# A recurrence feeding a GELU MLP: half of the inverse decay powers as ScalarE products, the decays' transfer issued by ScalarE, and one bonus half moved to VectorE

## The chip, the cores and the metric

The kernel runs on one core of a Trainium2 chip. The time is device time in microseconds (us) from the first to the last instruction of one launch; the median of several launches is compared. All work is in float32; a float32r product is split into a high and a low part, so that three matmuls stand for one.

## The reference

A linear recurrence over 768 positions for 4 batches and 8 heads of 48 channels, and then an MLP of 384 to 2048 to 384 with GELU on the 3072 tokens that come out:

```python
for t in range(S):
    kt, vt, rt = (k[:, :, t], v[:, :, t], r[:, :, t])
    cur = np.einsum('bhd,bhe->bhde', u[None] * kt, vt)
    y[:, :, t] = np.einsum('bhd,bhde->bhe', rt, state + cur)
    state = w[None, :, :, None] * state + np.einsum('bhd,bhe->bhde', kt, vt)
...
h = x @ w_in
g = 0.5 * h * (1.0 + erf(h * inv_sqrt2))
return (g @ w_out).astype(np.float32)
```

## The kernel before

**Tiling.** The 768 positions are cut into 6 chunks of 128. In each chunk the 8 heads go as 4 pairs (in the order 3, 0, 1, 2), so there are 24 groups of one pair and one chunk. Inside a group the recurrence is matrix work: r and k are scaled by positive and negative powers of the decay w (tile Ts for the first four groups, Tb scaled by E for the later ones), their products give scores (bank A or Y in PSUM), the entries of the past are copied by a mask into Am (L489, L670), the diagonal is the bonus u·k·r (RK, cs, then "bonus": L415 on ScalarE, four activations for a half, or L420 on VectorE, one product for a half), and Am times v gives y. Between chunks a state (Sa, Sb) is carried.

**Prologue.** wu_sb holds the decays w and the bonus u. `powers` (L321 to L327, VectorE) makes w^1 to w^64 of all four pairs in W by doubling. `inverse` (L333, VectorE) makes w^-64 to w^-1 of one pair as one reciprocal of 112x64. `state_powers` (L346, L344, ScalarE) makes the powers up to w^128, which are flipped by TensorE into WN (L354, L357). RK is r times k (L465), Ts is T times the powers of W (L459), raw holds the MLP's packed weights, and E (four transfers, L366) is read back out of W.

**MLP.** The 96 steps (6 chunks of 16 blocks of 128 hidden units) each take 9 matmuls of 128x512 into bank Hp (L696; step 1 uses bank O2), two GELU evaluations on ScalarE (gh L728, gf L729), a subtraction on VectorE (gl = gf - gh, L730), and 9 matmuls into the three banks O (L740). "Hp wh" and "Hp wl" are the products with the high and the low part of the weights, three matmuls each. In the first chunk the weights are unpacked beside it, for each step j: wa (L395) and wb (L398) on ScalarE from raw, their sum wb (L400) on VectorE, wh (L404) on ScalarE, wl (L407) on VectorE. "products" of a group (L606 old states, L614 scores A<-Tb, L623 gains A<-Nb, L634 new) is one block on TensorE; the states (L663) on VectorE need its gains, and the next group's block needs those states.

**What sets the order.** Every operation is handed to a class `Plan` with a modelled length, a due time and what it reads and writes. `run` plays a list schedule on these models, engine by engine, the earliest due operation that is ready first, and emits the instructions in that order; the engines then run their own streams in order and wait on semaphores. So any modelled cost, and any operation moved from one engine to another, can move others. All loads go through the queue of SyncE (SP), in the order of the plan; a load waits there for the landing of the load eight before it. `warm_up` puts HEATS matmuls of zeros on TensorE at the start, and the plan puts further such matmuls into modelled gaps until MLP step 0.

Of the kernel before, what the change touches and what calls it, by code (L numbers as in the profile page):

```python
# [9 lines left out]
F32 = mybir.dt.float32  # L10
# [6 lines left out]
AF = mybir.ActivationFunctionType  # L17
# [6 lines left out]
C = 128  # L24
NCH = S // C
PAIRS = (3, 0, 1, 2)
NP = H // 2
NB = B
TOK = NB * C
NJ = DF // 128  # L30
HALF = 64
# [7 lines left out]
LATER = 10 ** 7  # L39
FIRST, STEP, STEP_LAST = 27000, 8400, 3900  # L40
WEIGHT_AHEAD, GROUP_AHEAD, GROUP_DUE = 26000, 28000, 18000
LEFT = 6
HEATS, HEAT_NS, HEAT_ROOM, MM = 10, 300, 100, 233
WIDE = 96
POOL_DUE, POOL_CLASH = 8000, 550
LATER_BONUS = "d"
# [4 lines left out]

SCALE = ("dd", "d", "d", "d")
PRODUCT = ("d", "d", "d", "d")
BONUS = ("aa", "aa", "aa", "ad")


class Plan:
# [6 lines left out]
    LAG = {"pe": 220, "act": 140, "dve": 115, "pool": 90, "sp": 0, "do": 0}  # L64
    DMA_GAP, DMA_LEAD, DMA_FIXED, DMA_LANES = 480, 1050, 950, 8
    DMA_EARLY, DMA_RATES = 5000, (400.0, 345.0)
    DMA_QUEUED, DMA_SPREAD = 1200, 1050

    def __init__(self, after):
        self.after = after  # L70
# [3 lines left out]
    def add(self, eng, ns, at, fn, r=(), w=(), port=False):  # L74
        n = len(self.ops)
        deps = set()
        for x in r:
            deps.add(self.writer.get(x))
            self.readers.setdefault(x, []).append(n)
        for x in w:  # L80
            deps.add(self.writer.get(x))
            deps.update(self.readers.pop(x, ()))
            self.writer[x] = n
        deps -= {None, n}
        self.ops.append((eng, ns, at, fn, deps, port or eng == "pool"))
        self.reads.append(set(r))
        self.writes.append(set(w))
        return n

    def dma(self, nbytes, at, fn, r=(), w=()):  # L90
        self.add("sp", nbytes, at, fn, r, w)
# [18 lines left out]
    def play(self, due):  # L110
# [6 lines left out]
        bus, locked, lanes = 0.0, {"dve": 0.0, "pool": 0.0}, [0.0] * self.DMA_LANES  # L117
# [4 lines left out]
        for _ in ops:  # L122
            best, clash = None, float("inf")
            for e in self.LAG:
# [4 lines left out]
                while wait and wait[0][0] <= start:  # L129
                    n = heapq.heappop(wait)[1]  # L130
                    heapq.heappush(can, (due[n], n))
                if can:
                    n = can[0][1]
                else:
                    start = wait[0][0]
                    n = min((due[n], n) for at, n in wait if at == start)[1]
# [8 lines left out]
            start, e, n = best  # L145
# [14 lines left out]
            if e == "sp":  # L160
                free[e] = start + self.DMA_GAP
                queued = bus - start - self.DMA_LEAD
                bus = max(bus, start + self.DMA_LEAD) + ns / self.DMA_RATES[start >= self.DMA_EARLY]
                end = bus + self.DMA_FIXED + self.DMA_SPREAD * (queued > self.DMA_QUEUED)
                lanes = lanes[1:] + [end]
            else:
                free[e] = end = start + ns
# [23 lines left out]
def rwkv_gelu_mlp(tc, rkT, rkv, wuT, uN, wmlp, r, k, vT, w, u, out):  # L191
    nc = tc.nc
    with ExitStack() as ctx:
# [73 lines left out]
            else:  # L267
                dma(C * 4608, at + 1, lambda: nc.sync.dma_start(N[s], rkv[gi]), r=r, w=[f"Nr{s}", f"Nk{s}", f"Nv{s}"])

        dma(5000, -10 ** 6, lambda: nc.sync.dma_start(wu_sb, wuT), w=["w_sb"])  # L270
        load_group(0, LATER)


# [55 lines left out]
                n *= 2  # L329
            return last  # L330

        def inverse(p0, p1):
            return nc.vector.reciprocal(out=W[:, p0:p1, 0:HALF], in_=W[:, p0:p1, C:HALF:-1])  # L333

        add("dve", 1500, 5, powers, r=["w_sb"], w=["P"], port=True)
        first = PAIRS[0]
        add("dve", 480, 6, lambda: inverse(first, first + 1), r=["P"], w=[f"W{first}"])
        for p in PAIRS[1:]:
            add("dve", 480, LATER, lambda p=p: inverse(p, p + 1), r=["P"], w=[f"W{p}"])


        def state_powers():
# [13 lines left out]
        def flipped(dst):  # L356
            return lambda: nc.scalar.copy(out=dst, in_=O[0].rearrange("s (p j x) -> s p j x", p=NP, x=64)[:, :, :, :D])  # L357

        add("act", 1700, LATER, state_powers, r=["P"], w=["WKs"])
        add("pe", 560, LATER, lambda: flip(lambda p: WKs[:, p, :]), r=["WKs", "ident"], w=["O0"])  # L360
        add("act", 400, LATER, flipped(WN), r=["O0"], w=["WN"])

# [380 lines left out]
        def moe2(m, at, dest):  # L743
# [27 lines left out]
            for i, (d, bank, a, b) in enumerate(parts):  # L771
# [8 lines left out]
                        out=o, in_=bank[:, a:b], mul=256.0), r=[banks[i]], w=[f"{R}{'' if last else i}"])  # L780
                if last:
                    dma(512 * (b - a), at + 2000, lambda d=d, a=a, b=b, o=o: nc.sync.dma_start(dest[d][:, a:b], o), r=[R])
            if not last:
                dma(128 * 6144, at + 20000, lambda: nc.sync.dma_start(
                    dest.rearrange("d p n -> p d n"), flat2(raw[0]).bitcast(F32).rearrange("p (d n) -> p d n", d=3)),
                    w=[f"raw0{i}" for i in range(3)])
# [221 lines left out]
```

## Time and profile before

| what | value |
|---|---|
| median of 3 launches | 478.93 us (478.65 to 478.95) |
| the profiled launch | 478.3 us, of which the profile's span is 476.6 us |
| TensorE busy | 469.2 us, 98% of the span |
| VectorE, ScalarE, GpSimd busy | 230.7, 181.8, 67.6 us |
| granted clock of TensorE | 1.00 |

The profile is of one launch; 1.7 us of it lie outside the span. Rows below name an engine (PE is TensorE's matmuls and PEld its weight loads, DVE VectorE, ACT ScalarE, POOL GpSimd, SPq the queue of SyncE), a line of the kernel, the operation, and the tile written and read. "x4" after a row is a run of four such instructions with no wait between, and the bracket behind a row is the time that the engine stood idle before it and what ended that.

### The profile page before, as it was taken

The page shows a single profiled execution, that of the slowest core. Times are in us where ns is not written, and L with a number is a line of the kernel's source. Part 1 is how long each engine was busy: PE and PEld are TensorE (multiplying, and loading weights), DVE is VectorE, ACT ScalarE, POOL GpSimd, SP SyncE. Part 2 cuts the span into 40 slices and gives each one's busy share as a digit, 9 for nine tenths or more (in the row PEclk, how much of TensorE's full clock was granted, in tenths as well). Part 3 has the DMA queues.
Part 4 walks back from the last instruction along what each step waited for, and adds up shares of the span by engine and source line. Part 5 has one row for each costly group of instructions (what it writes and reads, how often), then busy time and mean ns, then how long its engine had stood idle before and what let it go on. Part 6 is the DMA issues. An engine that isn't in the chain of part 4 may idle for free.

```text
span 476.6 us, 10284 instructions
## 1 busy us (share of the span) xinstructions
PE 469.2 (98%) x4525; PEld 378.3 (79%) x4525; DVE 230.7 (48%) x345; ACT 181.8 (38%) x333; POOL 67.6 (14%) x91
## 2 busy tenths in 40 slices
PE   8999999999999999999999999999999999999996
PEld 6767788888888787888888888888888887888875
DVE  7989989754354266153543543544435311211111
ACT  9998897233222223222223222223322222322221
POOL 1331021221020222010202202202112000000000
PEclk9999999999999999999999999999999999999999
DMA  8978682414023034031231330321402000100002
GB/s 306 362 296 312 231 265 91 122 48 155 25 83 106 2 114 153 1 106 39 69 106 67 96 99 9 106 54 52 162 15 91 14 0 12 66 1 1 1 0 72
DMA packets 15426, 46.60 MB, mean 98 GB/s; under 512 B 3664, under 2 KB 4048, under 8 KB 15376
## 3 DMA queue, kind: packets, MB, share of 16 engines
q1 hardware_dynamic: 15376, 45.88, 28.8%
q8 instruction: 37, 0.61, 0.5%
q14 instruction: 13, 0.11, 0.1%
HBM read 38.73 MB, written 4.72 MB: 91 GB/s over the span
## 4 chain that ended last, share of the span: by engine, by line
PE 92%; DMA 4%; ACT 3%; issue 0%; DVE 0%; ACTq 0%
PE Hp L696 42%; PE O L740 41%; PE Y L606 2%; DMA E<-W 2%; PE A L614 2%; PE Y L634 2%; PE A L623 1%; DMA raw<-in_wmlp_dram 1%; PE Y L740 1%; ACT W L344 0%; ACT Sa L530 0%; ACT wa L312 0%; ACT L291 0%; ACT wa L395 0%; ACT gh L728 0%; ACT gf L729 0%
## 5 line engine op out<-in xcount | busy, mean ns | idle before, releaser
L696 PE MATMUL Hp<-xx,wh 128*128 128x512 f32 x570 | 167.2, 401 | 0.0
L730 DVE TENSOR_TENSOR gl<-gf,gh 128x512 fp32r<-128x512 f32 x92 | 66.9, 727 | 166.4 <-ACT gf L729 166.1
L728 ACT ACTIVATE gh<-Hp 128x512 fp32r<-128x512 f32 x91 | 54.4, 598 | 213.9 <-PE Hp L696 213.8
L696 PEld LDWEIGHTS Hp<-xx,wh 128*128 128x128 f32 x570 | 104.4, 188 | 25.8 <-ACT gf L729 1.5
L696 PE MATMUL Hp<-xx,wl 128*128 128x512 f32 x285 | 82.1, 395 | 0.0
L740 PE MATMUL O<-gh,wh 128*128 128x512 f32 (+1 forms) x276 | 78.6, 391 | 0.5 <-ACT gf L729 0.5
L740 PE MATMUL O<-gh,wl 128*128 128x512 f32 (+1 forms) x276 | 78.6, 391 | 0.0
L740 PE MATMUL O<-gl,wh 128*128 128x512 f32 (+1 forms) x276 | 78.3, 390 | 0.0
L696 PEld LDWEIGHTS Hp<-xx,wl 128*128 128x128 f32 x285 | 53.6, 188 | 12.7
L740 PEld LDWEIGHTS O<-gh,wh 128*128 128x128 f32 x276 | 51.7, 188 | 13.5 <-ACT gf L729 0.9
L740 PEld LDWEIGHTS O<-gh,wl 128*128 128x128 f32 x276 | 51.2, 188 | 11.6
L740 PEld LDWEIGHTS O<-gl,wh 128*128 128x128 f32 x276 | 51.0, 188 | 11.4 <-issue 0.2
L729 ACT ACTIVATE gf<-Hp 128x512 f32<-128x512 f32 x95 | 56.3, 593 | 0.0
L561 POOL TENSOR_TENSOR Nb<-Nb 128x384 f32<-128x384 f32 x20 | 20.4, 1018 | 124.7 <-DMA Nb<-in_rkv_dram 75.4
L558 DVE TENSOR_TENSOR Tb<-Tb,E 112x1024 f32<-112x1024 f32 x20 | 25.4, 1268 | 2.3 <-DMA Tb<-in_rkT_dram 2.3
L663 DVE SCALAR_TENSOR_TENSOR Sb<-Sa,E,A 48x192 f32<-48x192 f32 x40 | 16.5, 413 | 18.1 <-PE A L623 17.5
L433 ACT CAST xx<-Y 112x512 fp32r<-112x512 f32 x15 | 8.8, 587 | 38.8 <-PE Y L634 38.7
L564 POOL TENSOR_TENSOR Nb<-Nb,WN 128x384 f32<-128x384 f32 x20 | 20.3, 1016 | 21.2 <-DVE wl L407 7.8
L567 POOL TENSOR_TENSOR Nb<-Nb,u_sb 128x384 f32<-128x384 f32 x20 | 20.3, 1013 | 17.8 <-DVE gl L730 12.5
L570 DVE TENSOR_REDUCE cs<-Nb 128x8 f32<-128x384 f32 x20 | 11.1, 553 | 18.1 <-POOL Nb L567 15.8
L644 POOL MEMSET done<- 1x1 f32 x19 | 1.7, 89 | 124.6 <-PE Y L606 124.6
L670 DVE COPY_PREDICATED Am<-past,A 128x512 f32<-128x512 uint32 x20 | 14.9, 747 | 7.0 <-PE A L623 6.8
(124 smaller groups left out, 388.9 us busy)
## 6 DMA issues: line engine op xcount, KB each, us to landing
raw<-in_wmlp_dram SPq DMA_DIRECT2D x16, 767.8 KB, 6.6
Nb<-in_rkv_dram SPq DMA_DIRECT2D x20, 576.0 KB, 5.6
Tb<-in_rkT_dram SPq DMA_DIRECT2D x20, 512.0 KB, 4.1
out_dram<-raw SPq DMA_DIRECT2D x5, 768.0 KB, 3.6
T<-in_rkT_dram SPq DMA_DIRECT2D x4, 512.0 KB, 5.0
xx<-x SPq DMA_DIRECT2D x30, 64.0 KB, 4.2
N<-in_rkv_dram SPq DMA_DIRECT2D x4, 384.0 KB, 7.0
out_dram<-raw SPq DMA_DIRECT2D x2, 256.0 KB, 2.1
```

Of the source, the lines that this page charges most:

```text
L558: add("dve", 1140, LATER, lambda: nc.vector.tensor_tensor(out=flat, in0=flat, in1=E[:, p, 0].rearrange("l h i -> l (h i)").unsqueeze(1).to ...
L561: add("pool", pool(DM), LATER, lambda: nc.gpsimd.tensor_tensor(out=n[:, 0], in0=n[:, 0], in1=n[:, 1], op=ALU.mult), r=[NK], w=[NR])
L564: add("pool", pool(DM), LATER, lambda: nc.gpsimd.tensor_tensor(out=kn, in0=kn, in1=WN2[:, p].rearrange("s j d -> s (j d)").unsqueeze(1).to ...
L567: add("pool", pool(DM), LATER, lambda: nc.gpsimd.tensor_tensor(out=n[:, 0], in0=n[:, 0], in1=u_sb[:, p, :].unsqueeze(1).to_broadcast([C, N ...
L570: add("dve", 465, LATER, lambda: nc.vector.tensor_reduce(out=sums, in_=n[:, 0].rearrange("s b (j d) -> s (b j) d", d=D), axis=AX.X, op=ALU ...
L663: add("dve", 430, at, lambda l=l, x=x: nc.vector.scalar_tensor_tensor(out=out[quarter(1 - x)], in0=src[l], scalar=E[l, p, 1, h, 32:33], in ...
L670: add("dve", 625, LATER, lambda: nc.vector.copy_predicated(out=am, mask=past2.bitcast(U32).unsqueeze(1).unsqueeze(1).to_broadcast([C, 2, N ...
L696: nc.tensor.matmul(dst, lhsT=wt[j][:, 0, k_ * 128:(k_ + 1) * 128], rhs=x[:, a, k_, :], start=start and k_ == ks[0], stop=stop and k_ == ks ...
L728: add("act", 480, LATER, lambda: nc.scalar.activation(out=high, in_=dst, func=AF.Gelu, scale=256.0), r=[H_], w=[GH])
L729: add("act", 480, LATER, lambda: nc.scalar.activation(out=gf, in_=dst, func=AF.Gelu, scale=256.0), r=[H_], w=["gf"])
L730: add("dve", dve(512), LATER, lambda: nc.vector.tensor_tensor(out=low, in0=gf, in1=high.bitcast(F32), op=ALU.subtract), r=["gf", GH], w=[G ...
L740: nc.tensor.matmul(dst[:, a:b], lhsT=wt[j][:, 1, d * 128:(d + 1) * 128], rhs=gt[:, a:b], start=(j == 0 and n == 0), stop=(j == NJ - 1 and ...
```

## The change

The diff is below. The lower half of the inverse powers is still a reciprocal, now of 112x32 (VectorE); the other half is that half times one column, w^-32, as an activation with a per-partition scale (ScalarE). All four pairs' are now in one order ahead of RK, `state_powers` reads them too in the plan's eyes (it waits for the products), the transfer of the decays is issued from ScalarE's queue ahead of everything else there, the third group's second bonus half goes to VectorE, one warm-up matmul is left out, and the plan's model of a large transfer is 550 ns longer. The output of the last chunk but one goes out as three transfers.

```diff
-HEATS, HEAT_NS, HEAT_ROOM, MM = 10, 300, 100, 233
+HEATS, HEAT_NS, HEAT_ROOM, MM = 9, 300, 100, 233
...
-BONUS = ("aa", "aa", "aa", "ad")
+BONUS = ("aa", "aa", "ad", "ad")
...
-    DMA_QUEUED, DMA_SPREAD = 1200, 1050
+    DMA_QUEUED, DMA_SPREAD, DMA_UNEVEN = 1200, 1050, 550
...
-                end = bus + self.DMA_FIXED + self.DMA_SPREAD * (queued > self.DMA_QUEUED)
+                end = bus + self.DMA_FIXED + (self.DMA_SPREAD if queued > self.DMA_QUEUED else self.DMA_UNEVEN * (ns > 200000))
...
-        dma(5000, -10 ** 6, lambda: nc.sync.dma_start(wu_sb, wuT), w=["w_sb"])
+        add("do", 1600, -10 ** 6, lambda: nc.scalar.dma_start(wu_sb, wuT), w=["w_sb"])
...
-        def inverse(p0, p1):
-            return nc.vector.reciprocal(out=W[:, p0:p1, 0:HALF], in_=W[:, p0:p1, C:HALF:-1])
+        def inverse(p, at):
+
+            add("dve", 300, at, lambda: nc.vector.reciprocal(
+                out=W[:, p, 32:HALF], in_=W[:, p, HALF + 32:HALF:-1]), r=["P"], w=[f"V{p}"])
+            add("act", 190, LATER, lambda: nc.scalar.activation(
+                out=W[:, p, 0:32], in_=W[:, p, 32:HALF], func=AF.Copy, scale=W[:, p, 32:33]), r=[f"V{p}"], w=[f"W{p}"])
...
-        first = PAIRS[0]
-        add("dve", 480, 6, lambda: inverse(first, first + 1), r=["P"], w=[f"W{first}"])
-        for p in PAIRS[1:]:
-            add("dve", 480, LATER, lambda p=p: inverse(p, p + 1), r=["P"], w=[f"W{p}"])
+        for n, p in enumerate(PAIRS):
+            inverse(p, LATER if n else 6)
...
-        add("act", 1700, LATER, state_powers, r=["P"], w=["WKs"])
+        add("act", 1700, LATER, state_powers, r=["P"] + [f"W{p}" for p in PAIRS], w=["WKs"])
...
-            if not last:
+            if t == NCH - 2:
+                for d in range(3):
+                    dma(128 * 2048, at + 20000, lambda d=d: nc.sync.dma_start(
+                        dest[d], flat2(raw[0]).bitcast(F32)[:, d * TOK:(d + 1) * TOK]), w=[f"raw0{d}"])
+            elif not last:
```

The order of the instructions moves on all engines up to about the 100th microsecond's work. ScalarE's stream from the blanking of wa (L312) to the first group's bonus stood so before:

```order
L312 COPY wa_133<-zeros 128x768
L346 COPY W<-W 112x4x32
L344 ACTIVATE W<-W 112x64 x4
L344 ACTIVATE W<-W 112x32 x4
L287 COPY diag_85<-diag 64x64
L287 COPY past_86<-past 64x64 x2
L475 COPY cs_117<-Hp 128x8
L415 ACTIVATE Am_113<-diag,cs_117 128x128 x8
```

And after the change (the file's lines are shifted by two from here on; L336 is the new product, L348 and L346 are `state_powers`):

```order
L312 COPY wa_133<-zeros 128x768
L336 ACTIVATE W<-W 112x32 x3
L287 COPY diag_85<-diag 64x64
L336 ACTIVATE W<-W 112x32
L287 COPY past_86<-past 64x64
L348 COPY W<-W 112x4x32
L346 ACTIVATE W<-W 112x64 x4
L346 ACTIVATE W<-W 112x32 x4
L477 COPY cs_117<-Hp 128x8
L287 COPY past_86<-past 64x64
L417 ACTIVATE Am_113<-diag,cs_117 128x128 x8
```

Four products now stand ahead of `state_powers` and of the first group's cs. The DMA of wu_sb and the table load are the first two rows of the same stream.

VectorE's stream around the first "products" block, before (gl_126 is of MLP step 0, wl_80 is the low weights of step 2, Tb_98 the next group's scaled tile, L663 the states):

```order
L730 TENSOR_TENSOR gl_126<-gf,gh_124 128x512
L558 TENSOR_TENSOR Tb_98<-Tb_98,E 112x1024
L730 TENSOR_TENSOR gl_127<-gf,gh_125 128x512
L407 TENSOR_TENSOR wl_80<-wb_136,wh_76 128x768
L663 SCALAR_TENSOR_TENSOR Sb<-Sa,E,A 48x192 x2
L663 SCALAR_TENSOR_TENSOR Sa<-Sb,E,A 48x192
L570 TENSOR_REDUCE cs_117<-Nb_111 128x8
L663 SCALAR_TENSOR_TENSOR Sa<-Sb,E,A 48x192
L577 TENSOR_TENSOR Am_113<-diag_85,cs_117 128x512
L400 ISA wb_134<-wb_134,wa_133 128x1536
```

And after:

```order
L732 TENSOR_TENSOR gl_126<-gf,gh_124 128x512
L579 TENSOR_TENSOR Am_113<-diag_85,cs_117 128x512
L560 TENSOR_TENSOR Tb_98<-Tb_98,E 112x1024
L665 SCALAR_TENSOR_TENSOR Sb<-Sa,E,A 48x192 x2
L672 COPY_PREDICATED Am_113<-past_86,A 128x512
L665 SCALAR_TENSOR_TENSOR Sa<-Sb,E,A 48x192 x2
L409 TENSOR_TENSOR wl_80<-wb_136,wh_76 128x768
L732 TENSOR_TENSOR gl_127<-gf,gh_125 128x512
L402 ISA wb_134<-wb_134,wa_133 128x1536
L402 ISA wb_135<-wb_135,wa_132 128x1536
```

The states and the past scores went ahead of step 2's low weights and of gl of step 1.

TensorE's stream from MLP step 2's high weights (wh_76) on, before (gh_125, gl_127 are of step 1, gh_124 of step 2):

```order
L696 MATMUL Hp<-xx_121,wh_76 128x512 x3
L696 MATMUL Hp<-xx_121,wl_80 128x512 x3
L696 MATMUL Hp<-xx_121,wh_76 128x512 x3
L740 MATMUL O_70<-gh_125,wh_75 128x512
...
L740 MATMUL O_72<-gl_127,wh_75 128x512
L740 MATMUL O_70<-gh_124,wh_76 128x512
...
L614 MATMUL A<-Tb_98 64x64 x16
L623 MATMUL A<-Nb_112 48x48 x16
L634 MATMUL Y<-Am_113,Nb_111 48x64 x16
L696 MATMUL Hp<-xx_121,wh_77 128x512 x3
```

And after:

```order
L698 MATMUL Hp<-xx_121,wh_76 128x512 x3
L742 MATMUL O_70<-gh_125,wh_75 128x512
...
L616 MATMUL A<-Tb_98 64x64 x16
L625 MATMUL A<-Nb_112 48x48 x16
L636 MATMUL Y<-Am_113,Nb_111 48x64 x16
L698 MATMUL Hp<-xx_121,wl_80 128x512 x3
L698 MATMUL Hp<-xx_121,wh_76 128x512 x3
L742 MATMUL O_70<-gl_127,wh_75 128x512
...
L742 MATMUL O_70<-gh_124,wh_76 128x512
...
L698 MATMUL Hp<-xx_121,wh_77 128x512 x3
```

On ScalarE the casts wh (L406) of steps 3 and 4 now stand right ahead of gh of step 2. The second "products" block now stands inside step 2's Hp chain, so that step 2's GELU comes behind it; the rows left out are the other two banks O, the products with wl and, ahead of L616, the 16 products L608 with the old states. The first such block (L614 and L623 of Tb_97 and Nb_111), which stood right ahead of step 2's Hp, moved up by five matmuls, ahead of step 0's products with gl.

## Rows read from the trace of the kernel before

**Rows 1.** The page's first part: busy time and share of each engine.

```profile
PE 469.2 (98%) x4525; PEld 378.3 (79%) x4525; DVE 230.7 (48%) x345; ACT 181.8 (38%) x333; POOL 67.6 (14%) x91
```

**Rows 2.** Busy time of each engine by stretch, granted clock, DMA share, GB/s.

```profile
5.00:15.00 10.00, 9.49 (x97) 7.65 (x96) 9.61 (x14) 9.58 (x36) 0.00 (x0) 1.00 1.03 415
35.00:60.00 25.00, 25.00 (x225) 19.52 (x224) 24.08 (x32) 22.22 (x32) 3.91 (x6) 1.00 0.75 263
```

**Rows 3.** Timeline of SyncE's queue: start, length, line, transfer issued.

```profile
0.81 0.41 SPq L270 DMA_DIRECT2D wu_sb<-in_wuT_dram  x1
1.28 1.36 SPq L264 DMA_DIRECT2D T<-in_rkT_dram  x3
```

**Rows 4.** Timeline of VectorE from the decays' landing to the first masked copy.

```profile
2.43 0.17 DVE L322 TENSOR_SCALAR W<-wu_sb 112x4 f32<-112x4 f32 x1 [0.91 <-DMA wu_sb<-in_wuT_dram]
4.08 0.55 DVE L333 RECIPROCAL W<-W 112x64 f32<-112x64 f32 x1
5.08 0.69 DVE L465 TENSOR_TENSOR RK<-T 112x512 f32<-112x512 f32 x1 [0.45 <-DMA T<-in_rkT_dram]
5.69 1.37 DVE L333 RECIPROCAL W<-W 112x64 f32<-112x64 f32 x3
6.98 1.22 DVE L459 TENSOR_TENSOR Ts<-T,W 112x512 f32<-112x512 f32 x2
10.24 1.30 DVE L489 COPY_PREDICATED Am<-past,A 128x1024 f32<-128x1024 uint32 x1 [0.30 <-ACT Am L415]
```

**Rows 5.** Timeline of VectorE, 16 to 25 us.

```profile
16.85 0.69 DVE L420 TENSOR_TENSOR Am<-diag,cs 128x512 f32<-128x512 f32 x1
17.66 0.96 DVE L400 CUSTOM_DVE_ANT_0 wb<-wb,wa 128x1536 uint16<-128x1536 uint16 x1
23.43 1.37 DVE L400 CUSTOM_DVE_ANT_0 wb<-wb,wa 128x1536 uint16<-128x1536 uint16 x1
```

**Rows 6.** Timeline of ScalarE to the end of the first bonus.

```profile
4.60 0.29 ACT L346 COPY W<-W 112x128 f32<-112x128 f32 x1
4.79 1.91 ACT L344 ACTIVATE W<-W 112x64 f32<-112x64 f32 x8
7.70 2.45 ACT L415 ACTIVATE Am<-diag,cs 128x128 f32<-128x128 f32 x8
```

**Rows 7.** Timeline of ScalarE and TensorE around MLP step 1 (weights raw2).

```profile
23.76 0.59 ACT L433 CAST xx<-O 128x512 fp32r<-128x512 f32 x1 [0.52 <-PE O L503]
24.88 1.09 ACT L395 ACTIVATE wa<-raw 128x768 f16<-128x768 bf16 x1 [0.52 <-DMA raw<-in_wmlp_dram]
25.84 0.80 ACT L404 CAST wh<-wb 128x768 fp32r<-128x768 f32 x1
26.89 0.86 PE L696 MATMUL O<-xx,wh 128*128 128x512 f32 x3
31.42 0.50 PE L740 MATMUL O<-gh,wh 128*128 128x512 f32 x1 [0.47 <-ACT gf L729]
```

**Rows 8.** Timeline, all engines, around MLP step 2.

```profile
29.43 1.22 DVE L558 TENSOR_TENSOR Tb<-Tb,E 112x1024 f32<-112x1024 f32 x1
32.28 0.95 DVE L407 TENSOR_TENSOR wl<-wb,wh 128x768 fp32r<-128x768 f32 x1
33.30 0.97 PE L696 MATMUL Hp<-xx,wh 128*128 128x512 f32 x3
33.44 0.86 DVE L663 SCALAR_TENSOR_TENSOR Sb<-Sa,E,A 48x192 f32<-48x192 f32 x2 [0.21 <-PE A L623]
35.70 0.60 ACT L728 ACTIVATE gh<-Hp 128x512 fp32r<-128x512 f32 x1 [0.17 <-PE Hp L696]
36.91 0.86 PE L740 MATMUL O<-gl,wh 128*128 128x512 f32 x3
37.75 0.76 DVE L670 COPY_PREDICATED Am<-past,A 128x512 f32<-128x512 uint32 x1
40.96 0.97 PE L696 MATMUL Hp<-xx,wh 128*128 128x512 f32 x3
```

## The prediction

> **What bounds the kernel now.** I read the page first: TensorE is busy for 469.2 of 476.6 us, 98% [rows 1]. So an edit can pay only where TensorE stands idle or does padding. The stretches say where: from 35 to 60 us it is busy for 25.00 of 25 us, and in the same stretch VectorE for 24.08 and ScalarE for 22.22; from 5 to 15 us VectorE has 9.61 of 10, ScalarE 9.58, and the transfer engines are at a share of 1.03 with 415 GB/s [rows 2]. The reader is to see two things. What the change can win lies in the first 33 us, where loads, VectorE and ScalarE are all full and TensorE waits for each in turn. Behind that, from 35 to 60 us, TensorE runs without a gap, but only just: VectorE, which feeds it, has 0.92 us to spare in 25. There the order of the work can lose, not win.
>
> The last waits of the prologue are MLP step 1, which starts at 26.89 when ScalarE has unpacked raw2 (it stood idle 0.52 us for that transfer, until 24.88), and a wait of 0.47 us at 31.42 for gf of step 1 [rows 7]. Step 2 then starts at 33.30 [rows 8], and from there TensorE stays full.
>
> **The loads.** With wu_sb gone from SyncE's queue the first T can be issued at 0.81 and not 1.28 [rows 3]; as the transfers run at their full share, every load behind it can land up to 0.47 us earlier, raw2 at 24.41. No load can gain more from this. Bounds: 0 if the stream starts when it did, 0.47 if not. I take 0.47.
>
> **VectorE.** The reciprocals took 0.55 + 1.37 = 1.92 us [rows 4]; a later one of 112x64 costs 1.37/3 = 0.46. At half the columns one costs between 0.23 (all by columns) and 0.46 (none); I take 0.28, so four cost 1.1 us, and 0.8 is saved. The 0.45 us in which VectorE stood before RK, waiting for T [rows 4], is filled too. The third group's bonus half adds one product of 0.69 [rows 5]. In all VectorE's list is 0.1 us shorter, and 0.56 with the wait.
>
> **ScalarE.** It gains a transfer's issue, 0.41 on SyncE [rows 3] (bounds 0 to 0.47), and four products; by the nearest row, 1.91/8 = 0.24 each in `state_powers` [rows 6], 0.96 together. It loses four bonus activations at 2.45/8 = 0.31 [rows 6], 1.2 us, but those stand late, near 18 us, and the additions stand at 1 to 6 us. `state_powers` began at 4.60 and the first bonus at 7.70; both move by 0.41 + 0.96 = 1.37, less the one small copy that now stands behind cs (about 0.25), so the first bonus ends near 11.3 and not 10.15 [rows 6]. The first masked copy on VectorE already waited 0.30 us for that bonus and started at 10.24 [rows 4]; it now starts near 11.4. VectorE has filled the time with RK and Ts of the third group, which stood behind that copy. Between the copy and the first sum wb at 17.66 [rows 5] there lay 7.42 us; less one RK (0.69) and one Ts (1.22) [rows 4], plus the new product (0.69), there lie 6.2: wb starts at 17.6. **The head start of the reciprocals is used up there**: 0 for TensorE. If ScalarE, which has wb's input to make after the same bonuses, is later, wb goes to 18.2.
>
> **Steps 0 and 1.** From the first wb to the end of the second one lie 24.80 - 17.66 = 7.14 us [rows 5], the same seven operations in the same order: the second sum is done between 24.8 and 25.4. Step 1 needs it and raw2. ScalarE starts wa of raw2 at 24.41; the next operation starts 0.96 after it (24.88 to 25.84); the copy xx (0.59), which stood ahead of raw2, now stands between, so wh begins at about 25.9 and step 1 at 26.7 to 26.9, against 26.89 [rows 7]: level. The moved copy eats the earlier load.
>
> Step 0's last third now stands behind step 1's three matmuls, so step 0's gelu and gl come 0.7 to 1.3 us later; the first "products" block (about 1 us) was put into that hole. It also stands ahead of the wait of 0.47 us. I put step 2 at 33.3, level; bounds 32.4 (the loads' 0.47 and the wait's 0.47 both won) and 33.7.
>
> **The second products block.** Here a stall goes to a new place. Before, step 2 ran whole, then step 1's nine matmuls, then six of step 2's, then the block. Now the block stands after three matmuls of step 2 and six of step 1. Three matmuls take (36.91 - 33.30)/5 = 0.72 us [rows 8], so TensorE is at the block at 33.3 + 3 x 0.72 = 35.5. The block needs the four state updates. VectorE comes to them after gl of step 0, the diagonal product (0.69) and Tb (1.22); Tb began at 29.43 and would begin near 31.9, so the states begin near 33.1, against 33.44, and with the past scores between them they take 0.86 + 0.76 + 0.86 = 2.5 [rows 8]: done at 35.6. **Wait of 0.2** (0 to 0.5).
>
> The block takes 40.96 - (36.91 + 3 x 0.72) = 1.9 us [rows 8]. Six matmuls of step 2's Hp follow, to 35.7 + 1.9 + 1.4 = 39.0. Then TensorE has only step 1's gl products, 0.72, to lie over step 2's gelu of 0.60 [rows 8]; before, it had nine matmuls, 2.2 us. And ScalarE has wh of steps 3 and 4 ahead of that gelu, which need two sums from VectorE; those stand behind the states, wl (0.95), gl (0.69, as any product of 512 columns) and come at 0.96 each [rows 5, 8]: 35.6 + 3.56 = 39.1. The second wh takes 0.80 [rows 7], to 39.9, the gelu 0.60, to 40.5, and TensorE was free at 39.75. With the usual overlap of 0.1 us between neighbours I take **a wait of 0.55** (0.05 if wh comes in time, 0.75 if nothing overlaps).
>
> **The sum.** The useful work on TensorE is the same, and the reordered pieces cancel by 41 us. Step 2 level (-0.9 to +0.4), +0.2, +0.55, and before there was no idle time to set against it (25.00 of 25). The warm-up matmul left out, the split output (not in the last chunk) and the reshuffled steps up to 100 us I put at 0; for the last the bound is +0.5, the room that VectorE lacks. Sum: +0.75. The profiled launch took 478.3, which makes 479.05; it lies 0.63 under the median, to which the measurement will be held, so I predict **478.93 + 0.75 = 479.7 us**.
>
> **The rivals.** *The loads win* (faster). Nothing in the rows forbids ScalarE and VectorE to keep up; then step 2 starts at 33.30 - 0.47 - 0.47 = 32.4 with no new wait: 478.0. It decides at step 2: before 32.9 with the states done before TensorE comes to the block. For it speaks that VectorE's list is shorter; against it, that ScalarE, as full, gets 1.37 us at the front. Chance 0.26, of which 0.17 beyond 0.2%.
>
> *The decays land late* (slower). All of VectorE's work waits for wu_sb, at 2.43 [rows 4], and until now nothing else ran on the transfer engines then, since T was issued 0.47 us behind it. Now both start together. The 112 rows of wu_sb are some 7 on each of 16 engines; if one 4 KB row of T goes between any two, at 415/16 = 26 GB/s [rows 2] that is 0.16 us each, 1.1 in all, and VectorE starts at 3.5. The slack is that between the second sum (24.8 to 25.4) and wh (25.9), about 0.5; the rest, 0.6, comes on top of my sum: 480.3. It decides at a landing of 2.9. Chance 0.22.
> The Trainium skill bears on this (DMA: Bandwidth & Descriptors, "Issuing engines are not separate DMA queues" and "Queues, rings and completion order"): transfers issued by different engines end up on the same 16 engines, which take turns between the queues packet by packet, and issuing from a second engine saves sequencer time alone. By that rule this rival is the case, and the sum would be +1.35; no run here shows wu_sb and T side by side, so I take the landing at 2.43 to 2.9 and leave the rule its chance.
>
> *Hidden anyway*: step 2 level and both waits covered, since VectorE is 0.5 us earlier at the states: 478.9. Chance 0.12.
>
> **How the numbers follow.** My forecast has the rest, 0.40, with 479.2 to 480.2 as its own range. About 0.2%, 0.96 us, is what a measurement of this kernel can tell from none. Faster: 0.17. Same: 0.09 of the first rival, 0.12, and 0.23 of the forecast, 0.44. Slower: 0.17 of the forecast and 0.22, 0.39. The range goes from 478.0, where the first rival's better half lies outside, to 480.7, which holds most of the late landing: one in ten is left out on either side.
>
> **What would show it.** In the changed kernel's trace: T issued at 0.81; wu_sb landed by 2.9; four reciprocals of about 0.28; first bonus ending near 11.3; the first wb at 17.6 to 18.2; step 1 at 26.9; step 2 at 33.3; a wait of TensorE ahead of the second products block, put down to the states, and one of about half a microsecond ahead of step 2's O products, put down to gh. I am wrong if step 2 starts before 32.9, if ScalarE has gh of step 2 ready in time, or if the trace shows gaps on TensorE behind 41 us that were not there before.

## The result, and the profile after

The changed kernel takes 484.64 us (median of 7 launches, 480.96 to 486.4) against 478.93 (7 launches, 478.65 to 484.54). It is slower: the medians differ by 5.71 us, 1.2%, and the ratio over all launches, with its 95% interval, is 1.0093 [1.0066, 1.012]. The launches do not lie around one value: one is at 480.96, the other six lie from 482.93 to 486.4. The profiled launch is the fastest, 480.96, with a span of 479.2. Its trace therefore shows only the first part of the loss, 2.6 us against the span of before; the rest had to be found in other launches.

The first part of the page, then the same columns as in [rows 2] for the same two stretches:

```profile
PE 470.7 (98%) x4526; PEld 378.9 (79%) x4526; DVE 229.0 (48%) x346; ACT 181.2 (38%) x333; POOL 68.5 (14%) x91
```

```profile
5.00:15.00 10.00, 8.28 (x74) 6.49 (x75) 9.25 (x21) 8.29 (x34) 0.00 (x0) 1.00 1.03 408
35.00:60.00 25.00, 24.43 (x342) 18.96 (x341) 24.38 (x35) 21.79 (x32) 4.47 (x7) 1.00 0.82 271
```

From 5 to 15 us TensorE is busy 1.21 us less than before and ScalarE 1.29 less, with the transfer engines as full as they were; from 35 to 60 us TensorE now has gaps, 0.57 us. The timeline of the prologue, all engines:

```profile
0.81 1.34 SPq L264 DMA_DIRECT2D T<-in_rkT_dram  x3
0.81 0.41 ACTq L270 DMA_DIRECT2D wu_sb<-in_wuT_dram  x1
...
4.83 0.17 DVE L322 TENSOR_SCALAR W<-wu_sb 112x4 f32<-112x4 f32 x1 [3.31 <-DMA wu_sb<-in_wuT_dram]
...
5.57 1.05 PE L305 MATMUL Hp<-zeros 128*128 128x512 f32 x2
6.36 0.98 DVE L334 RECIPROCAL W<-W 112x32 f32<-112x32 f32 x4
6.74 0.75 ACT L336 ACTIVATE W<-W 112x32 f32<-112x32 f32 x3 [1.61 <-DVE W L334]
...
7.94 1.13 PE L472 MATMUL Hp<-wu_sb,RK 112*128 112x96 f32 x8 [1.32 <-DVE RK L467]
...
10.56 2.45 ACT L417 ACTIVATE Am<-diag,cs 128x128 f32<-128x128 f32 x8
...
13.11 1.30 DVE L491 COPY_PREDICATED Am<-past,A 128x1024 f32<-128x1024 uint32 x1 [0.55 <-issue]
...
19.43 0.96 DVE L402 CUSTOM_DVE_ANT_0 wb<-wb,wa 128x1536 uint16<-128x1536 uint16 x1
```

T is issued at 0.81, as the diff would have it, and the four reciprocals cost 0.98 us. But the decays, issued at 0.81 in both kernels, reach VectorE at 4.83 and not at 2.43 [rows 4]. TensorE ends its warm-ups (the matmuls of zeros, L305) at 5.57 + 1.05 = 6.62 and then stands idle for 1.32 us until RK. In the kernel before, the last warm-up ends at 6.06 and the first real matmul (the first one on data) follows without a gap:

```profile
5.57 0.49 PE L305 MATMUL Y<-zeros 128*128 128x512 f32 x1
5.90 1.06 PE L470 MATMUL Hp<-wu_sb,RK 112*128 112x96 f32 x8
```

The view of the transfers says what lay in the decays' way. Queues (packets, megabytes, share) and the issue of wu_sb (KB, median us to landing), from 1.2 to 4.8 us after the change:

```profile
q1 hardware_dynamic: 242, 0.93, 69.7%
q10 hardware_dynamic: 128, 0.01, 2.3%
...
wu_sb<-in_wuT_dram ACTq DMA_DIRECT2D x1, 5.2 KB, 4.0
```

And the same issue in the kernel before, from 1.2 to 3.8 us:

```profile
wu_sb<-in_wuT_dram SPq DMA_DIRECT2D x1, 5.2 KB, 1.6
```

The 128 packets of wu_sb have a queue of their own now, q10, and stand beside 242 packets of SyncE's loads: 4.0 us instead of 1.6. In the records of single packets they run from 2.50 to 4.26, where before they ran alone from 1.84 to 2.08.

Timeline of ScalarE and TensorE from MLP step 1 on:

```profile
24.67 1.08 ACT L397 ACTIVATE wa<-raw 128x768 f16<-128x768 bf16 x1 [0.24 <-DMA raw<-in_wmlp_dram]
...
26.62 0.84 ACT L406 CAST wh<-wb 128x768 fp32r<-128x768 f32 x1 [0.37 <-DVE wb L402]
...
27.99 0.96 PE L698 MATMUL O<-xx,wh 128*128 128x512 f32 x3
...
34.48 0.85 PE L698 MATMUL Hp<-xx,wh 128*128 128x512 f32 x3
...
39.16 1.57 ACT L406 CAST wh<-wb 128x768 fp32r<-128x768 f32 x2
40.63 0.59 ACT L730 ACTIVATE gh<-Hp 128x512 fp32r<-128x512 f32 x1
...
41.27 0.97 PE L742 MATMUL O<-gh,wh 128*128 128x512 f32 x3 [0.38 <-ACT gh L730]
...
50.33 0.97 PE L742 MATMUL O<-gh,wh 128*128 128x512 f32 x3 [0.20 <-ACT gh L730]
```

Step 1 starts 1.10 us later than before (27.99 against 26.89 [rows 7]) and step 2 1.18 later (34.48 against 33.30 [rows 8]). Then come a wait of 0.38 ahead of step 2's O products and one of 0.20 two steps on. TensorE's last matmul ends at 474.76 instead of 472.10.

So two losses were to be explained: some 1.5 to 2 us that every launch has, and 2 to 5.5 more that most launches of the changed kernel have and its trace has not. Those launches, from 482 us up, are called long below.

### The profile page after: what moved, and what is told of

Read it like the earlier page. It is cut to its first block, busy times and chain, and to the rows that moved or that the text cites. A ratio compares the mean times of both kernels' runs of the same rounds, so it can differ in the third digit from the quotient of the medians.

```text
span 479.2 us, 10300 instructions
## 1 busy us (share of the span) xinstructions
PE 470.7 (98%) x4526; PEld 378.9 (79%) x4526; DVE 229.0 (48%) x346; ACT 181.2 (38%) x333; POOL 68.5 (14%) x91
## 4 chain that ended last, share of the span: by engine, by line
PE 90%; DMA 3%; ACT 2%; SPq 2%; DVE 2%; issue 0%
PE Hp L698 41%; PE O L742 40%; PE Y L608 2%; PE Y L636 2%; PE A L616 2%; PE A L625 1%; DMA Tb<-in_rkT_dram 1%; DMA raw<-in_wmlp_dram 1%; PE Y L742 1%; DMA wu_sb<-in_wuT_dram 1%; SPq L368 1%; ACT wa L397 0%; PE O L698 0%; ACT W L346 0%; ACT wh L406 0%; DVE wl L409 0%
## 5 line engine op out<-in xcount | busy, mean ns | idle before, releaser
L698 PEld LDWEIGHTS Hp<-xx,wh 128*128 128x128 f32 x570 | 104.4, 188 | 25.8 <-ACT gf L731 1.6
L560 DVE TENSOR_TENSOR Tb<-Tb,E 112x1024 f32<-112x1024 f32 x20 | 24.4, 1218 | 2.9 <-DMA Tb<-in_rkT_dram 2.9
```

Of the source, the lines that this page charges most:

```text
L560: add("dve", 1140, LATER, lambda: nc.vector.tensor_tensor(out=flat, in0=flat, in1=E[:, p, 0].rearrange("l h i -> l (h i)").unsqueeze(1).to ...
L698: nc.tensor.matmul(dst, lhsT=wt[j][:, 0, k_ * 128:(k_ + 1) * 128], rhs=x[:, a, k_, :], start=start and k_ == ks[0], stop=stop and k_ == ks ...
```

## The experiments

Each kernel was timed together with the kernel before; "before" below is the median of the latter in that measurement. Two theories stood at first. *The landing*: the late decays cost the time, by the delay itself or by what it does to TensorE. *The order*: what costs is the order of instructions that the plan puts out.

### The landing

**e1_wu_on_sync.** The changed kernel, its order kept; the transfer alone is issued by SyncE again, ahead of T.

```diff
-        add("do", 1600, -10 ** 6, lambda: nc.scalar.dma_start(wu_sb, wuT), w=["w_sb"])
+        wu_load = nc.sync.dma_start(wu_sb, wuT)
+        add("do", 1600, -10 ** 6, lambda: wu_load, w=["w_sb"])
```

> The changed kernel with one edit: the decays' transfer (wu_sb) is issued first on SyncE again; every engine's order of instructions is that of the changed kernel. Theory A (the decays land late because T's rows run beside them, and that is the cause of most of the loss): wu_sb lands at 2.4 us instead of 4.8, VectorE starts at 2.43, and what stays is the forecast's own sum plus the 0.47 us that the loads lose again: 479.3 to 480.4 us, with little scatter. Theory B (the new order and ScalarE's products cost most of it): still above 482 us.

480.96 (480.14 to 481.4, 7 launches; before 479.14), 1.0033 [1.0022, 1.0044]. All launches now lie within 1.3 us. The profiled launch is the longest of them, 481.4. Timeline, VectorE, ScalarE and TensorE:

```profile
2.49 0.17 DVE L323 TENSOR_SCALAR W<-wu_sb 112x4 f32<-112x4 f32 x1 [0.97 <-DMA wu_sb<-in_wuT_dram]
...
25.81 1.09 ACT L398 ACTIVATE wa<-raw 128x768 f16<-128x768 bf16 x1 [2.09 <-DMA raw<-in_wmlp_dram]
...
28.11 0.97 PE L699 MATMUL O<-xx,wh 128*128 128x512 f32 x3 [0.56 <-ACT wh L407]
```

The decays land as before, and 3.0 of the 4.8 us are gone that the changed kernel loses in the same measurement (e0 below). But step 1 is no earlier, 28.11, since raw2 lands at 25.8 in this launch. Some 1.8 us stay.

**e2_before_wu_on_act.** The kernel before, with that one transfer moved to ScalarE and nothing else.

```diff
-        dma(5000, -10 ** 6, lambda: nc.sync.dma_start(wu_sb, wuT), w=["w_sb"])
+        dma(5000, -10 ** 6, lambda: nc.scalar.dma_start(wu_sb, wuT), w=["w_sb"])
```

> The kernel before with one edit: wu_sb is issued by ScalarE's queue, SyncE starts with T. Theory A: wu_sb lands beyond 4 us, TensorE's chain starts about 2 us late, and the time is 1.5 to 6 us above the kernel before, with the scatter of the changed kernel. Theory B: wu_sb's place costs nothing, and the loads come 0.47 us earlier: 478.4 to 479.0 us.

484.48 (483.64 to 484.52, 4 launches; before 479.14), 1.0105 [1.009, 1.0119]. One word costs 5.3 us, more than the 2.1 us by which the decays are late (4.58 against 2.43). Here the profiled launch is a long one, and it shows why. Timeline of TensorE, then stretches (the column behind POOL is the granted clock):

```profile
4.72 0.80 PE L305 MATMUL A<-zeros 128*128 128x512 f32 x2
5.35 0.40 PE L305 MATMUL Y<-zeros 128*128 128x512 f32 x1
7.39 1.13 PE L470 MATMUL Hp<-wu_sb,RK 112*128 112x96 f32 x8 [1.64 <-DVE RK L465]
...
10.09 2.08 PE L484 MATMUL A<-Ts 64*128 64x128 f32 x16
```

```profile
7.50:10.00 2.50, 2.31 (x13) 1.61 (x13) 2.50 (x6) 2.40 (x11) 0.00 (x0) 0.70 1.02 413
10.00:12.50 2.50, 2.50 (x19) 2.19 (x19) 1.67 (x3) 2.15 (x8) 0.00 (x0) 0.50 1.05 420
...
15.00:17.50 2.50, 2.50 (x26) 2.25 (x24) 0.92 (x1) 1.80 (x7) 0.00 (x0) 0.50 1.22 330
...
20.00:22.50 2.50, 2.50 (x30) 2.01 (x28) 1.70 (x2) 2.50 (x9) 0.00 (x0) 1.00 1.02 354
```

After an idle 1.64 us TensorE starts its real work, and then falls to a granted clock of 0.50, the lower of its two levels (1.2 GHz): a block of 16 score matmuls takes 2.08 us, where the e5 profile below has 1.16 for the same block at full pace. It stays there from 8.5 until about 19 us, and VectorE and ScalarE wait for it (0.92 and 1.80 of 2.5 us busy from 15 to 17.5).

**e3_t_held.** The changed kernel; the first transfer of T waits for GpSimd's memset of `ones`, so that wu_sb gets ahead.

```diff
+                if gi == 0:
+                    after(ins, start[0])
...
+            start.append(nc.gpsimd.memset(ones, 1.0))
```

> The changed kernel with one edit: SyncE's first transfer (T) waits for GpSimd's first memset (ends at 1.01 us), so that T is issued some 0.3 us behind wu_sb, which stays on ScalarE's queue; all orders as in the changed kernel. Theory A: the decays' rows are through before T's begin, wu_sb lands by 2.6 us, and the time is 479.2 to 480.2 us, up to 0.2 us better than with wu_sb on SyncE. Rival C (ScalarE's queue is slow at the start whatever runs beside it, first rows at 2.5 us and not 1.84): wu_sb still lands beyond 3.5 us, and the time stays above 480.5 us.

481.25 (480.43 to 482.12, 5 launches; before 479.14), 1.0044 [1.0031, 1.0057]. Timeline of VectorE:

```profile
3.23 0.17 DVE L334 TENSOR_SCALAR W<-wu_sb 112x4 f32<-112x4 f32 x1 [1.71 <-DMA wu_sb<-in_wuT_dram]
```

T was issued at 1.04, 0.23 us later, and VectorE started at 3.23 instead of 4.83; in the records of packets the first one of wu_sb comes at 1.82, as early as on SyncE's queue (1.84). ScalarE still issues wu_sb here, so most of its delay, 1.6 of 2.4 us, comes from T starting beside it. So ScalarE's queue isn't slow by itself (rival C); but the landing lies between the 2.6 and the 3.5 us that were expected, and the time is above the first theory's 480.2.

**e0_after_again.** The changed kernel once more, measured together with e1, e2 and e3.

> The changed kernel itself, once more, for a second profile of it: its times run from 481.0 to 486.4 us and its first profile, with wu_sb landed at 4.81, is the fastest of them. Theory A: the scatter is that of the landing, so a slower launch shows wu_sb landing later than 4.81, by about as much as it is slower. Rival: the landing is 4.8 again and the extra time lies elsewhere, in stretches with a granted clock under 1.

483.96 (480.5 to 486.32, 7 launches; before 479.14), 1.0091 [1.0058, 1.0124]: three launches at 480.5 to 480.95 with a mean granted clock of 0.999 to 1.000, four at 483.96 to 486.32 with 0.984 to 0.989. The profiled one, 480.95, has the late landing too (4.58). So the landing is late in a short launch as well; what differs between these launches is TensorE's clock. The 14 launches of the changed kernel (here and in the result) bear this out: with a mean clock of 0.992 they take 482.93 and 483.66, with 0.988 or 0.989 from 483.96 to 485.61, with 0.984 486.32 and 486.4. Two long ones, 484.88 and 485.09, have 0.999; more on them behind e5.

**e4_more_warm_up.** The changed kernel with three more warm-up matmuls of zeros, which the plan does not know of.

```diff
-            for n in range(HEATS):
+            for n in range(HEATS + 3):
```

> The changed kernel with one edit: three more warm-up matmuls on TensorE that the plan does not know of (every other instruction keeps its place), so that TensorE is busy until about 8.1 us, when the late decays let it start. Clock theory (with the decays late TensorE stands idle from 6.6 to 7.9 us, and in some launches the granted clock then falls to its lower level for a while): the granted clock is 0.997 to 1.0 in all launches, none takes 484 us, and the median falls to 480.7 to 481.5 us. Rival (the launches of 484 to 486 us come from the transfers): the scatter stays, median 483 to 485 us.

480.42 (479.98 to 481.08, 11 launches; before 479.15), 1.0026 [1.0016, 1.0035]. **e4_again** is the same kernel, measured again on another chip:

> The changed kernel with the three more warm-up matmuls once more, as the base of the run beside it: 480.4 us, clock 0.998 to 1.0 in all launches, step 2 at 34.2.

480.18 (480.04 to 481.13, 11 launches; before 478.92), 1.0028 [1.0019, 1.0037]. Timeline of TensorE in the first of them:

```profile
5.57 1.05 PE L305 MATMUL Y<-zeros 128*128 128x512 f32 x2
...
6.78 0.63 PE L305 MATMUL Hp<-zeros 128*128 128x512 f32 x2
7.73 1.13 PE L472 MATMUL Hp<-wu_sb,RK 112*128 112x96 f32 x8 [0.32 <-DVE RK L467]
```

The decays still come late (4.59), yet none of the 22 launches is long any more, and the time is no longer than with the transfer back on SyncE. So the 2 to 6 us that the long launches take more go with the idle TensorE, not with the late landing as such. What the late landing costs by itself was not separated: ScalarE starts on raw2 at 24.71 here and at 25.81 in e1's profile, so earlier loads may make up for it.

**e5_less_warm_up.** The other way round: the kernel before, its transfers untouched, with three warm-ups fewer.

```diff
-            for n in range(HEATS):
+            for n in range(HEATS - 3):
```

> The kernel before with one edit: three warm-up matmuls fewer than the plan counts on, all orders kept, the decays landing at 2.4 us as before. TensorE then stands idle from about 4.5 to 5.9 us. Clock theory: some or all launches show a granted clock of 0.984 to 0.990 and take 482 to 486 us, though no transfer is late. Rival: 478.7 to 479.8 us in all launches.

480.25 (479.12 to 482.44, 12 launches; before 479.15), 1.0025 [1.001, 1.004]: eight launches at 479.12 to 480.37, four at 482.08 to 482.44. One of the four was profiled; TensorE's timeline:

```profile
3.44 1.48 PE L305 MATMUL O<-zeros 128*128 128x512 f32 x3
5.58 2.02 PE L470 MATMUL Hp<-wu_sb,RK 112*128 112x96 f32 x8 [0.66 <-DVE RK L465]
...
8.73 2.08 PE L484 MATMUL A<-Ts 64*128 64x128 f32 x16
...
17.70 1.16 PE L484 MATMUL A<-Ts 64*128 64x128 f32 x16
```

The decays landed at 2.41, and still every block goes at half pace until 16 us. So long launches come without the late transfer too, where TensorE stops early.

The warm-ups show something more. In every profile they begin at half pace: three take 1.48 us, a pair 1.05; in e4 the last pair takes 0.63, and in e2 the last one 0.40. The trace's own records of the clock begin with one of full pace, at 4.4 to 7.1 us in 15 of the 16 profiles and at 16.10 us in this one, and matmuls that run across it get faster there; the columns and means of the granted clock count the time ahead of that first record as 1.00. So in e2 TensorE had reached its full pace, at 5.08 us, and fell back at 8.50; in this launch of e5 it stopped at 4.92 us, before it had reached it, and got there only at 16.10. And a mean clock near 1.00 doesn't exclude half pace at the start: it reads 1.000 in all four long launches of e5, so the two long ones of the changed kernel with 0.999 may be of this kind.

Over all measurements, with the matmuls of zeros and the idle time ahead of the first real matmul in the profiled launch (the plan adds two matmuls of zeros to the changed kernel's 9, so that it has 11, one more than before):

| kernel | matmuls of zeros | idle, us | long launches |
|---|---|---|---|
| before | 10 | none | 1 of 94 (484.54; the rest up to 480.34) |
| e2, wu_sb on ScalarE | 10 | 1.64 | 4 of 4 |
| changed | 11 | 1.32 and 1.08 | 10 of 14 |
| e5, fewer warm-ups | 7 | 0.66 | 4 of 12 |
| e1, wu_sb on SyncE | 11 | none | 0 of 7 |
| e4, more warm-ups | 14 | 0.32 and 0.20 | 0 of 22 |
| e11 (below), as many as e4 | 14 | 0.92 | 0 of 8 |

Among the other kernels e3, e1b and e8 have one launch each above 482 (482.12, 482.12 and 482.74, of 5, 12 and 12) and e9, slower as a whole, two of 6; none of these was profiled, and what made them long is open. With the same 14 matmuls the idle time differs between launches, 0.20 to 0.92 us, since the warm-ups end sooner where the pace rises sooner: the idle time in one profile is not that of every launch.

### The order

What stays with either cure is +1.3 to +1.8 us. The next kernels ask which part of the change carries it.

**e6_halves_alone.** The kernel before with the halved reciprocals, the products and the new dependency of `state_powers` alone, planned anew.

```diff
-            return nc.vector.reciprocal(out=W[:, p0:p1, 0:HALF], in_=W[:, p0:p1, C:HALF:-1])
+            add("dve", 300, at, lambda: nc.vector.reciprocal(
+                out=W[:, p, 32:HALF], in_=W[:, p, HALF + 32:HALF:-1]), r=["P"], w=[f"V{p}"])
+            add("act", 190, LATER, lambda: nc.scalar.activation(
+                out=W[:, p, 0:32], in_=W[:, p, 32:HALF], func=AF.Copy, scale=W[:, p, 32:33]), r=[f"V{p}"], w=[f"W{p}"])
```

> The kernel before with one part of the change: half of the inverse powers by products on ScalarE (the plan orders anew). The forecast's theory (VectorE's 0.8 us are used up by the first bonus, which waits for ScalarE): 478.5 to 479.9 us, no gain. Rival (VectorE's head start carries through to MLP step 2): 477.5 to 478.3 us.

480.83 (480.15 to 481.76, 7 launches; before 479.15), 1.0034 [1.002, 1.0047]: slower than either expectation.

**e1b_all_but_wu.** The changed kernel with wu_sb's transfer as before in the plan too, planned anew.

```diff
-        add("do", 1600, -10 ** 6, lambda: nc.scalar.dma_start(wu_sb, wuT), w=["w_sb"])
+        dma(5000, -10 ** 6, lambda: nc.sync.dma_start(wu_sb, wuT), w=["w_sb"])
```

> The changed kernel with wu_sb's transfer on SyncE in the plan too, so that the plan orders anew for it (the first run with wu_sb on SyncE kept the changed kernel's order). If the cost that stays without the late decays (about 1.6 us in that run) is that of the particular order: 478.5 to 480 us. If it is the work moved to ScalarE: 480 to 481.5 us again.

480.37 (479.16 to 482.12, 12 launches; before 479.15), 1.003 [1.0017, 1.0044]. The launches spread over both expected ranges; the one of 482.12 has a mean clock of 0.994.

**e7_halves_old_order.** The kernel before, plan and order untouched; each reciprocal emits its half and then the product.

```diff
-            return nc.vector.reciprocal(out=W[:, p0:p1, 0:HALF], in_=W[:, p0:p1, C:HALF:-1])
+            half = nc.vector.reciprocal(out=W[:, p0:p1, 32:HALF], in_=W[:, p0:p1, HALF + 32:HALF:-1])
+            nc.scalar.activation(out=W[:, p0, 0:32], in_=W[:, p0, 32:HALF], func=AF.Copy, scale=W[:, p0, 32:33])
+            return half
```

> The kernel before, its plan and so its order untouched, with the reciprocals of 112x32 and the four products emitted in their place (the first product ahead of the state powers, three behind them). If the 1.3 to 1.7 us that stay of the loss are the new order's: 478.6 to 479.6 us, as the kernel before on this chip. If they are the halves' own, since ScalarE is later: 480 to 481 us, as with the halves under a new plan.

479.67 (479.18 to 480.47, 11 launches; before 479.11), 1.0012 [1.0002, 1.0021].

**e8_new_order_no_products.** e1's order and queue with whole reciprocals (112x64) and no products; the bonus half on VectorE and the split output stay.

```diff
-                out=W[:, p, 32:HALF], in_=W[:, p, HALF + 32:HALF:-1]), r=["P"], w=[f"V{p}"])
-            add("act", 190, LATER, lambda: nc.scalar.activation(
-                out=W[:, p, 0:32], in_=W[:, p, 32:HALF], func=AF.Copy, scale=W[:, p, 32:33]), r=[f"V{p}"], w=[f"W{p}"])
+                out=W[:, p, 0:HALF], in_=W[:, p, C:HALF:-1]), r=["P"], w=[f"V{p}"])
+            add("act", 190, LATER, lambda: None, r=[f"V{p}"], w=[f"W{p}"])
```

> The changed kernel's order with wu_sb on SyncE (as in the first run of that), but the reciprocals whole on VectorE (112x64) and no product on ScalarE. If the order is the cause: 480 to 481.3 us again. If ScalarE's four products are the cause: 478.7 to 479.6 us.

480.44 (479.94 to 482.74, 12 launches; before 479.11), 1.0031 [1.0019, 1.0042]. Timeline of ScalarE and TensorE:

```profile
25.76 0.56 ACT L435 CAST xx<-O 128x512 fp32r<-128x512 f32 x1
26.22 0.82 ACT L406 CAST wh<-wb 128x768 fp32r<-128x768 f32 x1
...
27.10 0.96 PE L698 MATMUL O<-xx,wh 128*128 128x512 f32 x3 [0.47 <-ACT wh L406]
...
33.74 0.88 PE L698 MATMUL Hp<-xx,wh 128*128 128x512 f32 x3
...
40.55 0.97 PE L742 MATMUL O<-gh,wh 128*128 128x512 f32 x3 [0.37 <-ACT gh L730]
...
50.49 0.97 PE L742 MATMUL O<-gh,wh 128*128 128x512 f32 x3 [1.07 <-ACT gh L730]
```

e7 and e8 cross the two suspects. The products in the old order cost 0.56 us; the new order without any product costs 1.33. The order, with the bonus half and the split output that e8 keeps, is the larger part, and the wait ahead of step 2's O products (0.37) comes with it, as does a longer one (1.07) two steps on.

**e9_bonus_alone** and **e10_plan_alone** are the kernel before, planned anew with one other part of the change each: the bonus half on VectorE, or the constants and the split output.

```diff
-BONUS = ("aa", "aa", "aa", "ad")
+BONUS = ("aa", "aa", "ad", "ad")
```

> The kernel before with one part of the change: the third group's second bonus half on VectorE (the plan orders anew). By the forecast VectorE pays 0.69 us near 17 us where it is full, and ScalarE wins 1.2: 478.5 to 479.8 us. If every new order costs about 1.5 us here: 480 to 481 us.

```diff
-HEATS, HEAT_NS, HEAT_ROOM, MM = 10, 300, 100, 233
+HEATS, HEAT_NS, HEAT_ROOM, MM = 9, 300, 100, 233
...
-    DMA_QUEUED, DMA_SPREAD = 1200, 1050
+    DMA_QUEUED, DMA_SPREAD, DMA_UNEVEN = 1200, 1050, 550
```

> The kernel before with the rest of the change: one warm-up matmul fewer, 550 ns on large transfers in the plan's model, and the last-but-one chunk's output in three transfers. By the forecast 0 for each: 478.7 to 479.6 us. If every new order costs about 1.5 us: 480 to 481 us.

e9: 481.87 (481.1 to 482.91, 6 launches; before 479.11), 1.0053 [1.0039, 1.0068]. e10: 480.64 (479.81 to 481.36, 8 launches), 1.003 [1.0019, 1.0041]. TensorE's timeline in e9, then in e10:

```profile
43.01 0.97 PE L740 MATMUL O<-gh,wh 128*128 128x512 f32 x3 [1.34 <-ACT gh L728]
```

```profile
41.11 0.96 PE L740 MATMUL O<-gh,wh 128*128 128x512 f32 x3 [1.35 <-ACT gh L728]
```

e6, e9 and e10, with one part of the change each and an order of their own, cost 0.3 to 0.5%, as much as all parts together without the long launches (0.3% in e1 and e4); their costs do not add. In e9 and e10 the largest wait behind 40 us is ahead of a GELU's products. Their traces have the parts and the orders at once, so that the order carries the cost is argued from e7 and e8 and not shown for each of them.

**e11_no_gpsimd_overlap.** In e4's trace two VectorE operations near step 1 take half as long again as elsewhere, while GpSimd runs a product. Here the two GpSimd products (of groups 4 and 5) are replaced by a memset of one element, which leaves those groups' values uncomputed.

```diff
-            add("pool", pool(DM), LATER, lambda: nc.gpsimd.tensor_tensor(
+            add("pool", pool(DM), LATER, lambda: nc.gpsimd.memset(n[0:1, 0, 0, 0:1], 0.0) if gi == 5 else nc.gpsimd.tensor_tensor(
...
-            add("pool", pool(DM), LATER, lambda: nc.gpsimd.tensor_tensor(
+            add("pool", pool(DM), LATER, lambda: nc.gpsimd.memset(kn[0:1, 0, 0:1], 0.0) if gi == 4 else nc.gpsimd.tensor_tensor(
```

> The changed kernel with the three more warm-up matmuls, and two of GpSimd's products left out (replaced by a write of one element): the fifth group's Nb by WN2 and the sixth group's first Nb product, which ran at 27.8 and 29.7 us beside VectorE's low weights of step 1 (1.45 us instead of 0.95) and the sum for step 2 (1.52 instead of 0.95). Two groups' values are left uncomputed by that. If this overlap makes step 2 late: those two take 0.95 each, step 2 starts 0.7 to 1.1 us earlier (33.1 to 33.6), and the time is 479.4 to 479.9 us. If not: step 2 stays at 34.2 and the time at 480.4.

480.42 (479.73 to 481.22, 8 launches; before 478.92), 1.0026 [1.0015, 1.0037]; e4_again, measured beside it, 1.0028. Timelines of e4_again, then of e11:

```profile
27.97 1.45 DVE L409 TENSOR_TENSOR wl<-wb,wh 128x768 fp32r<-128x768 f32 x1
...
34.26 0.85 PE L698 MATMUL Hp<-xx,wh 128*128 128x512 f32 x3
```

```profile
27.92 0.94 DVE L409 TENSOR_TENSOR wl<-wb,wh 128x768 fp32r<-128x768 f32 x1
...
34.13 0.89 PE L698 MATMUL Hp<-xx,wh 128*128 128x512 f32 x3
```

The operation is shorter by 0.51 us, but step 2 starts only 0.13 earlier, and the time does not move. That the overlap carries the rest of the loss falls with this.

## Why the prediction was wrong

The forecast was 479.7 with a range to 480.7; the median is 484.64. The step that failed is the last of the rival *The decays land late*, where I chose: "I take the landing at 2.43 to 2.9". It was 4.58 to 4.83. A second step failed with it, the price of a late landing: 0.6 us by way of VectorE, 480.3 in all, where TensorE's idle time ahead of the first real matmul goes with 2 to 6 us in 10 of 14 launches.

- **The landing.** The rival itself was the case, and at 22% I gave it too little. In its direction the Trainium skill was right (DMA: Bandwidth & Descriptors, "Issuing engines are not separate DMA queues" and "Queues, rings and completion order": engines' transfers share the 16 engines, which take turns between queues by packets). The traces agree: beside T the decays reach VectorE at 4.83 (changed kernel) and 4.58 (e2), with T held back 0.23 us at 3.23 (e3). The size was off too: I added 7 x 0.16 = 1.1 us for turns with T's rows, and the measured delay is 2.2 to 2.4. In the packet records the first packet comes 0.66 us later than before (2.50 against 1.84), and the 128 take 1.76 us instead of 0.24.
- **What a late landing costs.** Here the chain of my reasoning went the wrong way. I followed the delay through VectorE to step 1 and priced it at 0.6 us. It went through TensorE's clock: the gap behind the warm-ups, and then half pace for some 10 us. e2 (transfer alone, +5.3 us), e4 (gap filled, landing still late, 22 launches within 481.13) and e5 (fewer warm-ups, landing in time, 4 of 12 launches long) show it from three sides. The warm-up matmul left out, which I put at 0, did not make the gap: the plan put in two others, and the warm-ups of the changed kernel end later than before, at 6.62 against 6.06.
- **First bonus and first wb.** 13.01 (10.56 + 2.45) and 19.43 against 11.3 and 17.6 to 18.2: both late, with the decays. With these in time (e1) they are 10.87 and 18.48, near the forecast.
- **Step 1, called level.** It came 1.10 us late. ScalarE could start on raw2 at 24.67, 0.21 earlier than before and not 0.47; xx went in ahead of wh as forecast; wh then stood 0.37 us for the second sum. In e8, with the decays in time and T issued as before, raw2 came at 24.80, and the copy xx ahead of wh alone put step 1 at 27.10, 0.21 late. In no trace did the loads win.
- **Step 2 and the wait of 0.47 ahead of it.** Between steps 1 and 2 the new order lost 0.08 us, so "level" holds from there.
- **The second products block.** A wait of 0.2 forecast, none seen.
- **Ahead of step 2's O products.** The place and the releaser (gh, behind the casts wh of steps 3 and 4) were right: 0.38 in the changed kernel, 0.37 to 0.38 in e0, e1, e4, e6, e8 and e11, against 0.55. A second one of 0.20 at 50.33 was not forecast; it is 1.07 in e8.
- **Right as priced.** T's issue at 0.81; reciprocals 0.98/4 = 0.25 each (0.28) and products 0.75/3 = 0.25 (0.24).
- **The sum without the landing.** +0.75 was forecast for the new order; e1, e4 and e8 measure +1.3 to +1.8. In e4, with the decays late, step 2 starts at 34.24, 0.94 late, and waits of 0.37 and 0.31 follow; in e8, with the decays in time, it starts at 33.74, 0.44 late, and waits of 0.37 and 1.07 follow. The term was right in sign and too small in size: step 2, which I had called level, is late, and a second wait of TensorE comes behind the one forecast.

**What stays open.** In e4 and e5 the number of warm-ups and the length of the gap change together; which of them decides was not separated. The gap's length alone does not: in e11 it was 0.92 us, and none of 8 launches was long, while e5 has 4 of 12 with 0.66 in the profiled one. Nor does any run show why one launch keeps its pace and another of the same program does not. None of the changed kernel's long launches was profiled: that they went at half pace is read from e2 and e5, and from the clocks of eight of the ten (0.984 to 0.992). One launch of 94 of the kernel before was as long, though its profile, of another launch, has no gap. And which piece of the new order costs how much was not separated: e6, e9 and e10 each make another order, and no run has the old order with the bonus half moved.

## What to carry to other kernels

A transfer of a few KB that everything waits for goes onto the queue ahead of the large ones, not beside them on a second queue: 0.47 us of issue time saved cost 2.4 us of landing. Where warm-up matmuls keep TensorE busy until the first data come, a later arrival has to be paid for with more of them; look at the idle time ahead of the first real matmul and at the lengths of the matmuls around it, in a long launch too. And where a list schedule sets the order, price an edit by the order that comes out: here each small part, planned anew, cost 0.3 to 0.5%, and the four products in the old order about 0.1%.

## What the runs showed of the hardware

A small transfer's packets were stretched from 0.24 to 1.76 us by a stream on another queue (changed kernel against before). TensorE's warm-ups began at half pace in all 16 profiles, and the first record of full pace comes at 4.4 to 7.1 us in 15 of them. In e2's profiled launch TensorE fell back to half pace, at 8.5 us, after a gap of 1.64 us, and stayed there for some 10 us though it was busy throughout (2.50 of 2.50 us in the stretches from 10 to 17.5). In e5's profiled launch, one of 4 long ones among 12 of the same program, it stopped at 4.92 us at half pace and did not reach full pace before 16.10. The granted clock reads 1.00 before that although blocks take 2.08 us and not 1.16, because the clock's records begin only at 16.10. A VectorE operation on 128x768 took 1.45 us beside a GpSimd product and 0.94 without it, at the same place (e4_again, e11).
